# Doubled tails for the on-chip transposes, moved b2 sums and a held-back QK product in a fused attention and MLP kernel

## The chip, the cores and the metric

The kernel runs on one NeuronCore of a Trainium2 chip. The metric is the device time of one launch in microseconds (us). Work is spread over TensorE (PE: matmuls, with its weight loads shown as PEld), VectorE (DVE), ScalarE (ACT), GpSimd (POOL) and SyncE (SP), which here only issues DMAs. Every engine runs its own instructions strictly in the order in which they stand, and waits for other engines through semaphores: an instruction that waits holds up everything behind it on its engine.

## The reference

One transformer block over 2048 rows of 576 columns. Attention has 32 heads of 18 columns; each row looks at eight rows, itself and those 2, 4, ... 14 rows back.

```python
qkv = layernorm(x) @ wqkv                               # 576 -> 3 x 576
logits = einsum("bhsd,bhswd->bhsw", q, kg) * scale       # kg: k at s, s-2, ..., s-14
o = einsum("bhsw,bhswd->bhsd", softmax(logits), vg) @ wo
h = x + o
h2 = h + gelu(layernorm(h) @ w1 + b1) @ w2 + b2          # 576 -> 4608 -> 576
```

## The kernel before

The rows are split into 16 tiles of 128, tile j holding rows j, j + 16, j + 32 and so on, so that the eight rows of a window lie in tiles of the same parity at the same partition (or one partition up, which is what the "halo" copies supply). Even tiles are projected first, then odd ones. Attention takes the tiles in the order 14, 12, 10, ... 0, 15, ... 1, two at a time; these pairs are the groups: group 0 is tiles 14 and 12, group 1 is 10 and 8, group 2 is 6 and 4, group 3 is 2 and 0. All engines but the DMA rings follow an order that is written out by hand; pools only add the waits.

*Projection* (`qkv_duo`, line 297; matmuls at L216). 24 visits of two products each. A product has a first phase and a second; the second waits for a marker, a GpSimd no-op that itself waits for the first phase (L226), so **markers stand in GpSimd's queue** with everything else there. PSUM pairs A, B and C go round; a product can begin when ScalarE has emptied the pair used three products earlier (L311). Pair D takes transposes and the output product `wo_duo`. The tables `after`, `between` and `hooks` say what each engine gets behind, inside and within a visit.

*Transposes on TensorE* (`transpose_in`, L181). For groups 0's two tiles, the attention output o (`tr_o`) and the normalized h (`tr_h`) are turned in 64-row halves: five 128-column blocks, two matmuls each. The fifth block starts at column 448, and as its lower 64 rows of output must hold columns 512 to 575 once more, two more matmuls of 64 x 64 follow. `tr_x` leaves these two out. From group 1 on, the same turning is done by DMA: a store to the DRAM tile `td` (L198, L199), then a transposing read (L204 and L434 for o into `oT`, L498 for normalized h into `hnT`).

*Attention on VectorE.* For a tile: QK product (L343, `att_qk_a`), four halving additions (L352, `att_qk_add`) and one more into `logits` (L359), maximum and subtraction (L365, L366), on ScalarE the exponential (L384), denominators (L392 to L394), PV product (L398), additions (L404), last one into `q_all` (L405), which then holds o. `halo(j, 1)` and `halo(j, 2)` (L338, issued by SyncE) bring rows of k and v into the ring slot of tile j. They overwrite what the QK or PV product of that tile has read, so they wait for it; they also wait for the store of tile j to DRAM (`store_halo`, L295).

*LN2 of group 0* (`ln2`, L147 to L170): statistics on VectorE, the power -0.5 on GpSimd (L161), `ln_nmr` on VectorE (L170), normalization on ScalarE (L174). `add_b2` (L504) writes h + b2 on VectorE to `x_all`, where the output is summed. *LN2 from group 1 on* (`ln2_act`, L479 to L483, and `ln2_send`): statistics on ScalarE, the power on GpSimd (L482). `root` can make the next QK product wait for that power (lines 345 to 347); it is set for every tile but those of group 1.

*MLP.* `mlp1` multiplies a group's `hnT` by w1 in four visits (L216, `pm`), ScalarE applies gelu (L562), `mlp2` multiplies by w2 (L581 for groups 0 and 1; from group 2 on `mlp2_fast`, L669, with a scheme of seven products for eight, whose sums VectorE makes at L639 and L649). While group k runs here, attention of group k + 2 and LN2 of group k + 1 run beside it. For k = 0 the tables call tiles c = 10, d = 8, e = 6, f = 4; for k = 1 c = 6, d = 4, e = 2, f = 0. `ia` and `ib` are lists of calls put ahead of a row of `mlp2` of the group's first and second tile, `m1[v]` of a visit of `mlp1`.

SyncE's queue for k = 0, `ia[19]`, is in this order: `put_b2` of tile 8, stores of tiles 4 and 2 to DRAM, `halo(4, 1)`, then the store of tile 8's normalized h to `td`, then the two transposing reads into `hnT`:

```python
ia[19] = [lambda d=d: wo_visit((d, "A"), fill=True), c_(ln2_h, d), c_(ln2_act, d), c_(put_b2, d), c_(att_qk_a, f),
          c_(halos, 2), c_(halo, f, 1), c_(ln2_send, d), c_(ln2_ins, c, d), c_(att_qk_rest, f, 1), c_(exps, e, f)]
```

Of the kernel before, what the change touches and what calls it, by code (L numbers as in the profile page):

```python
# [17 lines left out]
def kernel(  # L18
# [157 lines left out]

    def transpose_in(pair, src, twice=True):
        def turn(rows, kt, c):
            for r in range(2):
                block = src[half_rows(r), c:c + P if rows.start is None else D]  # L180
                nc.tensor.matmul(pair[rows, r, kt * HP:(kt + 1) * HP], lhsT=block, rhs=ident[half_rows(r), half_rows(r)],  # L181
                                 start=True, stop=True, skip_group_check=True)

        for kt in range(KT):
            turn(slice(None), kt, min(kt * P, D - P))
        if twice:
            turn(half_rows(0), KF, KF * P)

# [76 lines left out]
    def tr_x(j, tag):  # L265
        pair = psum_pair(tag or "CAB"[(ring_pos[0] + 1) % 3], "xt_pt")
        transpose_in(pair, q_all[:, j, :], False)
# [26 lines left out]
    def store_halo(j, ts=slice(0, 2)):  # L294
        nc.sync.dma_start(out=kv_dram[j, 1:P + 1, ts, :], in_=kv_ring[j % 2][:, j // 2, ts, :])  # L295

# [42 lines left out]

    root = [None]  # L340

    def att_qk_a(j):
# [12 lines left out]
    def att_qk_b(j, i, skip=0):  # L355
        side[j] = i
        out = logit_of([j])[:, 0]
        att_qk_add(j, ((0, 0, 9), (0, 0, 4), (0, 0, 2), (0, 0, 1))[skip:])
# [63 lines left out]
    def tr_o(j, tag):  # L422
        pair = psum_pair(tag, "o_pt")
        transpose_in(pair, q_all[:, j, :])
        nc.scalar.copy(**turned(new_oT(j), pair))
# [4 lines left out]
    def send_o(j):  # L430
        o_sent[j] = dma_out(q_all[:, j, :])

    def read_o(j):
        nc.sync.dma_start_transpose(out=new_oT(j)[:], in_=o_sent.pop(j)[:])  # L434

# [39 lines left out]
    def ln2_act(j):  # L475
        h = h_of[j]
        y = sb.tile([P, D], BF16, tag="hn", name="hn", bufs=2)
        nmean, var, rstd = (sb.tile([P, 1], F32, tag=f"ln2_{t}", name=f"ln2_{t}", bufs=2) for t in ("nmean", "var", "rstd"))
        nc.scalar.activation(out=y[:], in_=h[:], func=ACT.Identity, scale=-1.0 / D, accum_out=nmean[:])  # L479
        nc.scalar.activation(out=y[:], in_=h[:], func=ACT.Square, bias=nmean[:], accum_out=var[:])  # L480
        nc.scalar.activation(out=var[:], in_=var[:], func=ACT.Identity, scale=(1.0 + EPS) / D, bias=eps2[:])  # L481
        ins = nc.gpsimd.tensor_tensor(out=rstd[:], in0=var[:], in1=mhalf[:], op=ALU.pow).ins  # L482
        root[0] = ins if j not in GROUPS[1] else None  # L483
        hn[j] = (h, rstd, nmean, y)
# [35 lines left out]

    def ln2_hn(j):
        h, rstd, nmr = hn[j]
        hn[j] = sb.tile([P, D], BF16, tag="hn", name="hn", bufs=2)
        ln_apply_act(hn[j][:], h[:], rstd[:, 0:1], nmr[:, 0:1])

    def hnT_slot(j):
# [5 lines left out]
    def tr_h(j, tag):  # L532
        pair = psum_pair(tag, "h_pt")
        transpose_in(pair, hn.pop(j)[:])
        nc.scalar.copy(**turned(hnT_slot(j), pair))
# [145 lines left out]
    def c_(fn, *a):  # L681
        return lambda: fn(*a)
# [100 lines left out]
    with tc.manual_schedule(engines={ENG.PE, ENG.Activation, ENG.DVE, ENG.SP, ENG.Pool}):  # L783
# [132 lines left out]
        for n, v in enumerate((19, 19, 20, 20, 21, 22)):  # L916
# [5 lines left out]
            3: [c_(ln1_even_rstd, 6, 7), c_(ln1_stats, 8)],  # L922
            4: [c_(ln1_rstd, 8), c_(ln1_stats, 9), c_(ln1_stats, 10, c_(ln1_bias, 8))],
            5: [c_(ln1_act, 8, 0), c_(ln1_rstd, 9), c_(ln1_bias, 9), c_(att_qk_a, A[0])],
# [7 lines left out]
            13: [c_(ln1_act, 10, 1), c_(in_x, 2), c_(out_x, 3)],  # L932
            14: [c_(att_pv, A[1]), c_(in_x, 3), c_(load, b2_bc, B_b2.partition_broadcast(P))],
            15: [c_(halo, A[1], 2)],
            17: [c_(ln2, A[0]), c_(att_qk_a, A[2])],
            18: [c_(ln2_rstd, A[0]), c_(add_b2, A[0]), c_(ln2_bias, A[0]), c_(halo, A[2], 1), c_(att_qk_add, A[2], ((0, 0, 9),))],
            19: [c_(ln2, A[1])],
            20: [c_(ln2_rstd, A[1]), c_(add_b2, A[1]), c_(ln2_bias, A[1]), c_(att_qk_rest, A[2], 0, 1)],
        }
# [3 lines left out]
            18: {1: [c_(tr_o, A[1], "D")]},  # L943
            19: [c_(ln2_hn, A[0])],
            21: [c_(ln2_hn, A[1])],
            22: [c_(att_exp, A[2])],
# [43 lines left out]
        def halos(n):  # L990
            for _ in range(min(n, len(pending_halo))):
                store_halo(pending_halo.pop(0))

# [11 lines left out]
        for k, g in enumerate(GROUPS):  # L1005
# [11 lines left out]
            if k == 0:  # L1017
                m1[0] += [c_(halos, 1), c_(load_w2, 6), c_(att_qk_a, d), c_(att_qk_rest, d, 1), c_(halo, d, 1)]
                mid[0] = {1: [c_(exps, d)]}
                m1[1] = [c_(pv_t, c), c_(pv_t, d), c_(att_qk_a, e), c_(halo, e, 1)]  # L1020
                late_wo = wo_duo(c, "B")
                ia[0] = [c_(ln2_h, c), c_(ln2_act, c), c_(put_b2, c), c_(ln2_send, c), c_(att_qk_rest, e, 0)]
                ia[19] = [lambda d=d: wo_visit((d, "A"), fill=True), c_(ln2_h, d), c_(ln2_act, d), c_(put_b2, d), c_(att_qk_a, f),
                          c_(halos, 2), c_(halo, f, 1), c_(ln2_send, d), c_(ln2_ins, c, d), c_(att_qk_rest, f, 1), c_(exps, e, f)]
                ib[0] = [c_(finish_out, g[0]), c_(out_sum, g[0]), c_(att_den, e, f), c_(pv_sum, e), c_(send_o, e)]
                ib[8] = [c_(read_o, e), c_(out_store, g[0])]
            elif k == 1:
                m1[0] += [c_(pv_sum, d), c_(send_o, d)]
# [100 lines left out]
```

## Time and profile before

| what | value |
|---|---|
| median of 3 runs | 361.9 us (361.39 to 362.56) |
| the profiled execution | 361.35 us, of which its span is 359.6 us |
| granted TensorE clock | 1.000 |
| busy: PE, PEld, DVE, ACT, POOL | 353.4, 292.4, 296.3, 234.8, 46.5 us |
| matmuls L216 pq (projection) | 864, 283 ns each, overlapping |
| transposes L181 of o and of h | 24 and 24, 190 ns each in 64 x 128 form, 213 ns in 64 x 64 form |
| b2 sums L504 | 2, 0.75 us each |
| power of LN2 (L161, L482) | 27 instructions, 22.6 us |

The span is the time from the first to the last instruction; 1.75 us of the profiled execution lie outside it. Matmuls are pipelined, so their durations overlap: the pace of TensorE is read from the distance between starts, not from the busy time. In the lines that follow the first number is the start in us from the start of the span and the second the length; a bracket gives the idle time of that engine just before, and what ended it.

### The profile page before, as it was taken

What the parts mean: (1) busy time and instruction counts of PE and PEld (TensorE: products, weight loads), DVE (VectorE), ACT (ScalarE), POOL (GpSimd) and SP (SyncE); (2) the same over time, 40 slices, a digit from 0 to 9 for tenths busy, and PEclk for the clock granted to TensorE, in tenths of its full rate; (3) what the DMA queues carried; (4) which work ended last, traced back from release to release, by engine and by line L of the source; (5) the groups of instructions that cost most, each with busy time, mean ns of one, the idle gap of its engine ahead of it and who ended that gap; (6) DMA issues with size and microseconds to landing.
All of it is one profiled execution on the core that took longest, in us unless ns stands there. A gap on an engine that the chain in (4) does not pass through costs nothing.

```text
span 359.6 us, 11560 instructions
## 1 busy us (share of the span) xinstructions
PE 353.4 (98%) x4942; PEld 292.4 (81%) x4942; DVE 296.3 (82%) x417; ACT 234.8 (65%) x519; POOL 46.5 (13%) x61
## 2 busy tenths in 40 slices
PE   7999999999999999999999999999999999999996
PEld 3778977887789877887788778877887788778874
DVE  5999999999989999997799899989998998520431
ACT  4879756897647783668566956695669566706620
POOL 2241004000112020201110202021102110210000
PEclk9999999999999999999999999999999999999999
DMA  7996789973447494731563655344636254273001
GB/s 241 339 285 192 202 223 300 369 246 73 136 88 119 142 239 81 137 71 51 94 101 76 98 124 85 90 96 110 88 90 100 57 86 58 54 122 50 4 1 33
DMA packets 62980, 46.29 MB, mean 129 GB/s; under 512 B 32192, under 2 KB 60736, under 8 KB 62928
## 3 DMA queue, kind: packets, MB, share of 16 engines
q1 hardware_dynamic: 58960, 41.50, 44.0%
q0 software_dynamic: 3744, 3.84, 9.8%
q8 instruction: 38, 0.62, 0.8%
q10 hardware_dynamic: 224, 0.22, 0.2%
q14 instruction: 14, 0.11, 0.1%
HBM read 23.38 MB, written 12.42 MB: 100 GB/s over the span
## 4 chain that ended last, share of the span: by engine, by line
PE 76%; DVE 14%; DMA 3%; SPq 2%; ACT 2%; issue 1%; POOL 0%; POOLq 0%; ACTq 0%
PE pm L216 34%; PE po L669 25%; PE pq L216 8%; PE po L581 5%; PE pw L216 4%; DVE prod L352 2%; DVE ln_stats L148 2%; DVE prod L343 2%; DVE prod L398 1%; DMA x_all<-in_A_x_dram 1%; DVE prod L404 1%; ACT h_all L562 1%; SPq L104 1%; DMA hnT<-td 1%; DMA oT<-td 1%
## 5 line engine op out<-in xcount | busy, mean ns | idle before, releaser
L216 PE MATMUL pm<-hnT,w_sb 64*128 64x256 bf16 x2304 | 143.0, 269 | 0.2 <-DMA hnT<-td 0.2
L562 ACT ACTIVATE h_all<-pm,b_sb 128x256 f16<-128x256 f32 (+1 forms) x288 | 108.6, 496 | 51.2 <-PE pm L216 50.6
L216 PEld LDWEIGHTS <-w_sb 64*128 64x128 bf16 x2304 | 113.6, 94 | 13.5 <-issue 1.9
L669 PEld LDWEIGHTS <-h_all 128*128 128x128 f16 x480 | 46.2, 98 | 13.7 <-issue 1.6
L216 PE MATMUL pq<-wq_sb,xnT 64*128 64x288 bf16 x720 | 54.9, 283 | 1.3 <-ACT xnT L272 0.5
L216 PEld LDWEIGHTS <-xnT 64*128 64x128 bf16 x864 | 44.0, 94 | 10.6 <-ACT xnT L272 1.2
L352 DVE TENSOR_TENSOR prod<-prod 128x2304 bf16<-128x2304 bf16 (+1 forms) x64 | 44.2, 691 | 2.0
L343 DVE TENSOR_TENSOR prod<-kv_ring,q_all 128x4608 bf16<-128x4608 bf16 x16 | 40.9, 2555 | 3.1 <-POOL ln_rstd L482 2.5
L398 DVE TENSOR_TENSOR prod<-kv_ring,probs 128x4608 bf16<-128x4608 bf16 x16 | 40.9, 2558 | 1.1 <-DMA kv_ring<-kv_dram 0.6
L216 PE MATMUL pm<-hnT,w1h_sb 64*128 64x256 bf16 x288 | 39.5, 269 | 0.0
L669 PE MATMUL po<-w2a_sb,h_all 128*128 128x288 bf16 (+1 forms) x262 | 35.8, 286 | 0.0
L404 DVE TENSOR_TENSOR prod<-prod 128x2304 bf16<-128x2304 bf16 (+1 forms) x32 | 33.9, 1058 | 1.1
L581 PEld LDWEIGHTS <-h_all 128*128 128x128 bf16 x288 | 27.9, 98 | 7.9 <-issue 1.0
L669 PEld LDWEIGHTS <-kv_ring 128*128 128x128 f16 x252 | 24.6, 98 | 6.3
L581 PE MATMUL po<-w2a_sb,h_all 128*128 128x288 bf16 x224 | 28.5, 286 | 0.0
L216 PE MATMUL pq<-wqh_sb,xnT 64*128 64x288 bf16 x144 | 27.6, 283 | 0.0
L771 POOL DMA_DIRECT2D x_all<-o_sb x12 | 10.7, 890 | 124.6 <-PE pw L216 71.8
L482 POOL TENSOR_TENSOR ln_rstd<-ln_var,mhalf 128x1 f32<-128x1 f32 x13 | 9.3, 718 | 81.9 <-ACT ln_var L481 81.9
L669 PE MATMUL po<-w2b_sb,h_all 128*128 128x288 bf16 (+1 forms) x122 | 19.7, 286 | 0.2 <-DVE h_all L649 0.2
L649 DVE TENSOR_TENSOR kv_ring<-h_all 128x1536 f16<-128x1536 f16 (+3 forms) x9 | 6.8, 761 | 15.6 <-ACT h_all L562 15.6
L216 PE MATMUL pw<-wo_sb,oT 64*128 64x288 bf16 x256 | 19.5, 283 | 0.1
L161 POOL TENSOR_TENSOR ln_rstd<-ln_veps,mhalf 128x1 f32<-128x1 f32 (+2 forms) x14 | 13.3, 965 | 47.6 <-DVE ln_veps L155 31.1
(107 smaller groups left out, 399.3 us busy)
## 6 DMA issues: line engine op xcount, KB each, us to landing
w_sb<-in_B_w_dram SPq DMA_DIRECT2D x6, 768.0 KB, 6.3
kv_ring<-kv_dram SPq DMA_DIRECT2D x28, 144.0 KB, 2.4
kv_dram<-kv_ring SPq DMA_DIRECT2D x13, 288.0 KB, 4.1
x_all<-in_B_b_dram SPq DMA_DIRECT2D x15, 144.0 KB, 3.7
w2a_sb<-in_B_w_dram SPq DMA_DIRECT2D x2, 1008.0 KB, 8.0
td<-q_all SPq DMA_DIRECT2D x14, 144.0 KB, 1.8
td<-hn SPq DMA_DIRECT2D x14, 144.0 KB, 1.8
x_all<-h POOLq DMA_DIRECT2D x14, 144.0 KB, 4.8
```

Of the source, the lines that this page charges most:

```text
L148: nc.vector.bn_stats(out=stats[:, i, c, :], in_=src[:, c * HALF:(c + 1) * HALF])
L161: nc.gpsimd.tensor_tensor(out=rstd[:], in0=veps[:], in1=mhalf[:].to_broadcast([P, n]), op=ALU.pow)
L216: last = nc.tensor.matmul(duo["g"][r ^ swap][i], lhsT=lhsT, rhs=rhs, start=(swap == 0 and i == 0 and kt == 0), stop=(swap == 1 and kt == K ...
L343: ins = nc.vector.tensor_tensor(out=prod[:], in0=k_ring[j % 2], in1=q_all[:, j, :].unsqueeze(1) .to_broadcast([P, W, D]), op=ALU.mult).ins
L352: nc.vector.tensor_tensor(out=prod[:, :, o * H:o * H + n], in0=prod[:, :, a * H:a * H + n], in1=prod[:, :, c * H:c * H + n], op=ALU.add)
L398: nc.vector.tensor_tensor(out=prod[:].rearrange("p w (d h) -> p w d h", h=H), in0=v_ring[j % 2].rearrange("p w (d h) -> p w d h", h=H), in ...
L404: nc.vector.tensor_tensor(out=prod[:, 0:n, :], in0=prod[:, 0:n, :], in1=prod[:, n:2 * n, :], op=ALU.add)
L482: ins = nc.gpsimd.tensor_tensor(out=rstd[:], in0=var[:], in1=mhalf[:], op=ALU.pow).ins
L562: pace[0] = nc.scalar.activation(out=hT(grp)[:, f, 0:N], in_=ps[:, r, i * N:(i + 1) * N], func=ACT.Gelu_apprx_tanh, bias=b1_sb[:, f:f + 1] ...
L581: nc.tensor.matmul(banks[half], lhsT=hT(grp)[:, f, i * P:(i + 1) * P], rhs=w2_rows(f)[:, half * HALF:(half + 1) * HALF], start=(f == 0), s ...
L669: nc.tensor.matmul(bank, lhsT=l, rhs=r, start=start, stop=stop, skip_group_check=True)
L771: nc.gpsimd.dma_start(out=x_of(j), in_=o_of.pop(j), accum_op=ALU.add)
```

## The change

The two extra matmuls of each of the four transposes of group 0 go. In their place somebody writes columns 512 to 575 twice into a new tile `tail`, from which the fifth block is turned: ScalarE for o of tile 14 (behind visit 14), VectorE for o of tile 12 (behind its PV sums), ScalarE for the two normalized h (a second normalization of 128 columns right behind the first). The two b2 sums move from group 0's LN2 to the place behind the PV sums of tile 8. In the second half of group 0's `mlp2` the sum h of tile 8 comes ahead of the last logits, maximum and subtraction of tile 6, and the QK product of tile 4 waits for the power of tile 8's LN2. In group 1, o of tile 4 is sent ahead of `halo(4, 2)`, the store of output tile 14 goes two visits later, and the seven stores of odd tiles wait for the transposing read of o. In the projection `ln_bias` of the first four odd tiles moves ahead of the last statistics. Numbers in `after` are visits.

```diff
-    def transpose_in(pair, src, twice=True):
-        def turn(rows, kt, c):
-            for r in range(2):
-                block = src[half_rows(r), c:c + P if rows.start is None else D]
-                nc.tensor.matmul(pair[rows, r, kt * HP:(kt + 1) * HP], lhsT=block, rhs=ident[half_rows(r), half_rows(r)],
-                                 start=True, stop=True, skip_group_check=True)
-        for kt in range(KT):
-            turn(slice(None), kt, min(kt * P, D - P))
-        if twice:
-            turn(half_rows(0), KF, KF * P)
+    def transpose_in(pair, src, tail=None):
+        for kt in range(KT):
+            c = min(kt * P, D - P)
+            block = tail[:].rearrange("p r c -> p (r c)") if kt == KF and tail is not None else src[:, c:c + P]
+            for r in range(2):
+                nc.tensor.matmul(pair[:, r, kt * HP:(kt + 1) * HP], lhsT=block[half_rows(r)],
+                                 rhs=ident[half_rows(r), half_rows(r)], start=True, stop=True, skip_group_check=True)
+    def twice(src):
+        return src[:, KF * P:D].unsqueeze(1).to_broadcast([P, 2, HP])
+    def new_tail(key):
+        tails[key] = qp.tile([P, 2, HP], BF16, tag="tail", name="tail", bufs=2)
+        return tails[key][:]
+    def o_tail(j, copy):
+        copy(out=new_tail(("o", j)), in_=twice(q_all[:, j, :]))
...
-        root[0] = ins if j not in GROUPS[1] else None
+        root[0] = ins if j != GROUPS[1][0] else None
...
-    def ln2_hn(j):
+    def ln2_hn(j, tail=False):
...
+        if tail:
+            ln_apply_act(new_tail(("h", j)), twice(h), rstd[:, 0:1], nmr[:, 0:1])
...
-            4: [c_(ln1_rstd, 8), c_(ln1_stats, 9), c_(ln1_stats, 10, c_(ln1_bias, 8))],
+            4: [c_(ln1_rstd, 8), c_(ln1_stats, 9), c_(ln1_bias, 8), c_(ln1_stats, 10)],
...
-            14: [c_(att_pv, A[1]), c_(in_x, 3), c_(load, b2_bc, B_b2.partition_broadcast(P))],
+            14: [c_(o_tail, A[0], nc.scalar.copy), c_(att_pv, A[1]), c_(o_tail, A[1], nc.vector.tensor_copy), c_(in_x, 3), c_(load, b2_bc, B_b2.partition_broadcast(P))],
...
-            18: [c_(ln2_rstd, A[0]), c_(add_b2, A[0]), c_(ln2_bias, A[0]), c_(halo, A[2], 1), c_(att_qk_add, A[2], ((0, 0, 9),))],
+            18: [c_(ln2_rstd, A[0]), c_(ln2_bias, A[0]), c_(halo, A[2], 1), c_(att_qk_add, A[2], ((0, 0, 9),))],
...
-            20: [c_(ln2_rstd, A[1]), c_(add_b2, A[1]), c_(ln2_bias, A[1]), c_(att_qk_rest, A[2], 0, 1)],
+            20: [c_(ln2_rstd, A[1]), c_(ln2_bias, A[1]), c_(att_qk_rest, A[2], 0, 1)],
...
         def halos(n):
             for _ in range(min(n, len(pending_halo))):
-                store_halo(pending_halo.pop(0))
+                ins = store_halo(pending_halo.pop(0))
+                if o_read[0] is not None:
+                    tc.add_manual_dep(ins, o_read[0].name, sync_dep, reason="stores behind the read of o")
...
-                m1[1] = [c_(pv_t, c), c_(pv_t, d), c_(att_qk_a, e), c_(halo, e, 1)]
+                m1[1] = [c_(pv_t, c), c_(pv_t, d), c_(add_b2, g[0]), c_(add_b2, g[1]), c_(att_qk_a, e), c_(halo, e, 1)]
-                ia[0] = [c_(ln2_h, c), c_(ln2_act, c), c_(put_b2, c), c_(ln2_send, c), c_(att_qk_rest, e, 0)]
-                ia[19] = [lambda d=d: wo_visit((d, "A"), fill=True), c_(ln2_h, d), c_(ln2_act, d), c_(put_b2, d), c_(att_qk_a, f),
+                ia[0] = [c_(ln2_h, c), c_(ln2_act, c), c_(put_b2, c), c_(ln2_send, c), c_(att_qk_add, e, ADDS)]
+                ia[19] = [lambda d=d: wo_visit((d, "A"), fill=True), c_(ln2_h, d), c_(ln2_act, d), c_(put_b2, d), c_(att_qk_rest, e, 0, 4), c_(att_qk_a, f),
...
-                ib[8] = [c_(read_o, e), c_(out_store, g[0])]
+                ib[8] = [c_(read_o, e)]
             elif k == 1:
-                m1[0] += [c_(pv_sum, d), c_(send_o, d)]
+                m1[0] += [c_(att_pv_sum, d), c_(send_o, d), c_(halo, d, 2)]
-                m1[3] += [c_(att_qk_a, f), c_(halo, f, 1), c_(att_qk_add, f, ((0, 0, 9), (0, 0, 4)))]
+                m1[3] += [c_(out_store, GROUPS[0][0]), c_(att_qk_a, f), c_(halo, f, 1), c_(att_qk_add, f, ADDS[:2])]
```

More of the change, by code (lines that the diff above doesn't have):

```diff
@@ L174, in ln_apply_act @@
         nc.scalar.activation(out=dst, in_=src, func=ACT.Identity, scale=rstd, bias=nmr)
-    def transpose_in(pair, src, twice=True):
-        def turn(rows, kt, c):
+    def transpose_in(pair, src, tail=None):
+        for kt in range(KT):
+            c = min(kt * P, D - P)
+            block = tail[:].rearrange("p r c -> p (r c)") if kt == KF and tail is not None else src[:, c:c + P]
             for r in range(2):
-                block = src[half_rows(r), c:c + P if rows.start is None else D]
-                nc.tensor.matmul(pair[rows, r, kt * HP:(kt + 1) * HP], lhsT=block, rhs=ident[half_rows(r), half_rows(r)],
-                                 start=True, stop=True, skip_group_check=True)
-        for kt in range(KT):
-            turn(slice(None), kt, min(kt * P, D - P))
-        if twice:
-            turn(half_rows(0), KF, KF * P)
+                nc.tensor.matmul(pair[:, r, kt * HP:(kt + 1) * HP], lhsT=block[half_rows(r)],
+                                 rhs=ident[half_rows(r), half_rows(r)], start=True, stop=True, skip_group_check=True)
+    tails = {}
+    def twice(src):
[5 more added lines that the diff above has]
+        copy(out=new_tail(("o", j)), in_=twice(q_all[:, j, :]))
     def turned(dst, pair, k0=0, k1=KT):
@@ L266, in tr_x @@
         pair = psum_pair(tag or "CAB"[(ring_pos[0] + 1) % 3], "xt_pt")
-        transpose_in(pair, q_all[:, j, :], False)
+        transpose_in(pair, q_all[:, j, :])
         if EVEN.index(j) % 2 == 0:
@@ L294, in store_halo @@
     def store_halo(j, ts=slice(0, 2)):
-        nc.sync.dma_start(out=kv_dram[j, 1:P + 1, ts, :], in_=kv_ring[j % 2][:, j // 2, ts, :])
+        return nc.sync.dma_start(out=kv_dram[j, 1:P + 1, ts, :], in_=kv_ring[j % 2][:, j // 2, ts, :]).ins
     def qkv_duo(j, t):
@@ L340 @@
     root = [None]
+    ADDS = ((0, 0, 9), (0, 0, 4), (0, 0, 2), (0, 0, 1))
     def att_qk_a(j):
@@ L357, in att_qk_b @@
         out = logit_of([j])[:, 0]
-        att_qk_add(j, ((0, 0, 9), (0, 0, 4), (0, 0, 2), (0, 0, 1))[skip:])
+        att_qk_add(j, ADDS[skip:])
         nc.vector.tensor_tensor(out=out, in0=prod[:, :, 0:H], in1=prod[:, :, 8 * H:9 * H], op=ALU.add)
@@ L423, in tr_o @@
         pair = psum_pair(tag, "o_pt")
-        transpose_in(pair, q_all[:, j, :])
+        transpose_in(pair, q_all[:, j, :], tails.pop(("o", j)))
         nc.scalar.copy(**turned(new_oT(j), pair))
@@ L431, in send_o @@
         o_sent[j] = dma_out(q_all[:, j, :])
+    o_read = [None]
     def read_o(j):
-        nc.sync.dma_start_transpose(out=new_oT(j)[:], in_=o_sent.pop(j)[:])
+        o_read[0] = nc.sync.dma_start_transpose(out=new_oT(j)[:], in_=o_sent.pop(j)[:]).ins
     pw_of, o_sent = {}, {}
@@ L533, in tr_h @@
         pair = psum_pair(tag, "h_pt")
-        transpose_in(pair, hn.pop(j)[:])
+        transpose_in(pair, hn.pop(j)[:], tails.pop(("h", j)))
         nc.scalar.copy(**turned(hnT_slot(j), pair))
@@ L943 @@
             18: {1: [c_(tr_o, A[1], "D")]},
-            19: [c_(ln2_hn, A[0])],
-            21: [c_(ln2_hn, A[1])],
+            19: [c_(ln2_hn, A[0], True)],
+            21: [c_(ln2_hn, A[1], True)],
             22: [c_(att_exp, A[2])],
```

## The prediction

> **What bounds the kernel now.** I read the chain of work that ended last first, then the engines' timelines around its joints. TensorE takes 76% of the chain and from 125.5 to 338 us it never pauses: a delay that reaches it there is added to the end, and a gain must come before 125 us.
>
> ```profile
> PE 76%; DVE 14%; DMA 3%; SPq 2%; ACT 2%; issue 1%; POOL 0%; POOLq 0%; ACTq 0%
> ...
> 93.92 2.48 DVE prod L343
> 96.42 1.37 DVE prod L352
> 97.79 0.32 SPq L338
> ...
> 98.21 0.98 SPq L198
> ...
> 102.15 2.92 DMA hnT<-td
> ...
> 105.21 15.66 PE pm L216 x284
> 120.87 2.85 DMA oT<-td
> ```
>
> The reader sees that group 1's MLP (105.21) waits for VectorE, then for SyncE's halo copy of tile 4 (97.79), then for tile 8's normalized h (98.21) and its transposing read.
>
> ```profile
> 12.53 0.31 PE L181 MATMUL xt_pt<-ident,q_all 64*128 64x64 bf16 x10
> 12.68 0.65 PE L216 MATMUL pq<-wq_sb,xnT 64*128 64x288 bf16 x8
> ...
> 45.26 0.67 PE L216 MATMUL pq<-wq_sb,xnT 64*128 64x288 bf16 x8
> 45.75 0.31 PE L216 MATMUL pq<-wqh_sb,xnT 64*128 64x288 bf16 x2
> 45.87 0.48 PE L181 MATMUL o_pt<-ident,q_all 64*128 64x64 bf16 x12
> 46.28 0.66 PE L216 MATMUL pq<-wq_sb,xnT 64*128 64x288 bf16 x7
> ```
>
> Ten transposes hold TensorE from 12.53 to 12.68 (0.15 us), twelve, two of them 64 x 64, from 45.87 to 46.28 (0.41 us).
>
> ```profile
> 45.16 0.46 DVE L405 TENSOR_TENSOR q_all<-prod 128x576 bf16<-128x576 bf16 x1
> ...
> 60.55 0.75 DVE L504 TENSOR_TENSOR x_all<-h,x_all 128x576 bf16<-128x576 f32 x1
> 61.75 0.16 DVE L170 SCALAR_TENSOR_TENSOR ln_nmr<-ln_mv,ln_rstd 128x1 f32<-128x1 f32 x1 [0.45 <-POOL ln_rstd L161]
> ```
> ```profile
> 44.38 1.19 ACT L311 ACTIVATE kv_ring<-pq 128x576 bf16<-128x576 f32 x2 [1.00 <-PE pq L216]
> ```
> ```profile
> 60.71 1.00 POOL L161 TENSOR_TENSOR ln_rstd<-ln_veps,mhalf 128x1 f32<-128x1 f32 x1 [3.62 <-DVE ln_veps L155]
> ...
> 96.03 0.76 POOL L482 TENSOR_TENSOR ln_rstd<-ln_var,mhalf 128x1 f32<-128x1 f32 x1 [4.50 <-ACT ln_var L481]
> ```
>
> o of tile 14 is there at 45.16 + 0.46 = 45.62, while ScalarE empties projection pairs from 44.38. The second b2 sum lies inside the wait for the power; VectorE has no other idle time from 19 to 101 us. Last, TensorE's own small waits:
>
> ```profile
> 83.59 0.48 PEld L216 LDWEIGHTS <-oT 64*128 64x128 bf16 x10 [0.35 <-DMA oT<-td]
> ...
> 123.76 1.46 PEld L216 LDWEIGHTS <-oT 64*128 64x128 bf16 x26 [0.39 <-DMA oT<-td]
> ```
>
> By starts TensorE loses 0.25 us at 83.6, 0.35 at 105.2 (rows end at 104.86) and 0.26 at 123.8 (at 123.50 it could go on).
>
> **Part 1, to 66.55 us.** Four turns lose 0.26 us each: 1.0 us. ln_bias ahead of statistics frees ScalarE 0.6 us earlier and ends a TensorE gap of 0.40 us at 25.20. Little of this stays. ScalarE's tail copy of tile 14 stands ahead of the two evacuations that begin at 44.38, and waits for 45.62. It costs 0.29 us by a line through ScalarE's rows of 36 and 256 columns (0.19 and 0.42 us, the bounds). The first evacuation (0.65 us) then begins near 45.87 and ends at 46.52; the product that starts at 45.26 needs that pair, so it starts near 46.55, 1.29 us late, whatever was won earlier. The shorter turn leaves +1.03 at 46.28. Now waits shrink. The second turn needed pair D from tile 14's sum h (VectorE, 52.92). VectorE's tail copy of tile 12 costs 0.2 (0.15 for its 1-column rows, 0.42 for 256 columns from PSUM): h ends at about 53.2, TensorE comes at 53.9, so no wait, and +0.68 after the shorter turn. The third turn was followed by 0.15 us behind a marker queued after the power; that goes, as does 0.26: +0.3. The fourth must wait for ScalarE's tail (0.29 behind hn), which also delays an evacuation that had 0.2 us to spare: +0.3 at 66.55 (0 to 0.6). The wait at 83.6 takes 0.25 of it: nothing lasting.
>
> VectorE's own chain matters more. The power of tile 12 took 1.00 us with a b2 sum beside it; four powers with no two-operand VectorE work beside them took 2.10 us, 0.53 each. I take 0.53, that being the state after the change: VectorE reaches this power 0.13 late: the tail copy waits for the end of o (52.25 instead of the overlapped 52.17) and takes its 0.2, and about 0.1 comes back because ln_nmr of tile 14 no longer stands behind a b2 sum. So the power runs from 60.84 to 61.37 and ln_nmr comes at 61.42 instead of 61.75: -0.33 (+0.13 if 1.00 stays). The Trainium skill, "SBUF — State Buffer", section "SBUF: two separate sides", says that a GpSimd operation reading SBUF and a VectorE one with two SBUF inputs exclude each other for their whole length; the 1.00 us row, ending 0.4 after the sum, fits. Without that rule, the shift would be the +0.13, and the total 0.46 higher, 363.1.
>
> **Part 2, 85 to 105 us.** Both b2 sums now stand in VectorE's busy stretch: 2 x 0.67 (starts one after the other) = 1.34. QK of tile 6: 85.45 - 0.33 + 1.34 = 86.46, +1.0. Sum h of tile 10: 88.93, ScalarE's LN2 of tile 10 (88.71 to 92.67 before, 3.96 us) ends at 93.67. Ahead of logits, sum h of tile 8 comes at about 92.5 (before 93.17), but ScalarE takes it up only at 93.67 (before 93.95): of the 0.67 us won by the swap 0.28 is left. The marker of tile 8's output product, queued behind tile 10's power (90.86 + 1.0), holds TensorE 0.2 us; the next wait hides it. Power of tile 8: 96.03 - 0.28 = 95.75, ready at 96.28. **Now QK of tile 4 waits for it**: 96.32 instead of 93.83. Behind it VectorE is late by 2.5 us, and SyncE's halo copy of tile 4, which overwrites what this product reads, can't be issued before its end: 96.32 + 2.55 + 0.03 = 98.90, where the store's landing set 97.79. Tile 8's h, ready at 97.7, is queued behind that copy: 99.32 instead of 98.21, +1.1. Its issue took 0.98 us where others of this form take 0.34; if the longer time came from the stores then landing, 0.64 is won back. So the read into hnT lands +0.47 to +1.1 later; between ends so far apart I take 0.8: TensorE starts at 106.0.
>
> What the hold-back buys is small: the power of tile 8 took 0.76, of which 0.23 above 0.53.
>
> **Part 3, from 105 us.** SyncE no longer has an output store and a halo copy ahead of the sending of tile 4's o. VectorE finishes this o at 114.70 + 2.5 = 117.2; the next halo copy waits for a QK product to 119.7, so the read can be issued at 120.1 and land at 122.95 (before 123.72). TensorE comes at 123.50 + 0.8: the wait of 0.26 goes, +0.54 is left. The seven stores, held to that landing, issue from 123 to 128.4 (before 122.13 to 127.5), the two output stores to 129.8, then come two loads; tile 6's h wants the queue at 131.64 + 2.2, so they cost nothing. VectorE, less its 0.29 us of waiting at 121.25, makes sums h of group 2 2.2 us late; the second read into hnT, issued at 137.4, is issued at 139.6 and lands 2.9 to 4.6 us later (both measured), 142.5 to 144.2; TensorE wants it at 143.21 + 0.54 = 143.75. Between 0 and 0.45, I take 0.15. After 162.4 VectorE had waited 2.12 us for TensorE, which takes up the 2.2. Sum: 0.8 - 0.26 + 0.15 = **+0.7**. On the profiled execution: 361.35 + 0.7 = 362.05; this execution lies 0.55 below the median, so by the median **362.6 us**.
>
> **Rivals.** *A, the VectorE delay reaches TensorE again.* The 2.5 us also move the exponential of tiles 6 and 4 (to 103.7), the copy of group 0's first output (to 106.4) and the GpSimd DMA behind it (1.05 us, to 107.8), and the marker that TensorE needs at 107.39 + 0.8 = 108.2 is queued behind that DMA: 0.4 us of cover where there were 2.2. If it starts 0.6 us after its release, as others do, 0.2 is lost; with the 1.1 end in part 2 and hnT at 144.2 or a little later, +1.5 to +2.2: about 363.8. For it: three small covers at once; against: each holds by itself at my mid values. *B, not slower:* the b2 sums and the hold-back end before SyncE needs tile 4's halo. Place: the copy at 97.79. It decides if QK of tile 4 ends by then, so starts by 95.2, 1.1 us earlier than I have. Then the store of tile 8's h goes at 98.2 or 97.9, the 0.35 at 105.2 shrinks, the 0.26 at 123.8 goes: 361.9 - 0.3 to 0.6, 361.4. Against: VectorE has no idle time in which 1.34 us of sums could hide. *C, the tail copy on ScalarE isn't absorbed:* if the power of tile 12 and the DMA of tile 10's o do not come earlier and ScalarE's evacuations stay crowded, 0.5 more reaches 83.6 us; but the wait at 105.2 hides what is below 0.8, so 362.9.
>
> **How the numbers follow.** Forecast 0.55 (own range 362.1 to 363.3), A 0.25, B 0.12, C 0.08. The median of three runs before spans 1.2 us, so within 0.3% (1.09 us: 360.8 to 363.0) is what can't be told from no change. The forecast lies three quarters within and one quarter above, A is above, B half below (runs differ) and half within, C half and half. Slower: 0.14 + 0.25 + 0.04 = 0.43; faster 0.06; same 0.51. Range 361.4 to 364.0: B's value below, A's end above.
>
> **What would show it.** Right: 10 transposes in 0.15 us; ScalarE idle up to a tail copy at 45.65 and TensorE idle over 0.8 us near 45; QK of tile 4 at about 96.3, released by GpSimd; halo copy of tile 4 near 98.9; first pm of group 1 near 106.0 on hnT; no wait for oT of tile 4. Wrong: QK of tile 4 before 95.2, or the store of tile 8's h ahead of 98.2; an hnT wait at group 2 over 0.5 us; TensorE gaps after 162 us.

## The result, and the profile after

The changed kernel takes 363.38 us (median of 7 runs, 362.37 to 363.5), the kernel before beside it on the same chip 361.57 us (361.25 to 362.56). The ratio is 1.0039, with a 95% interval of 1.0025 to 1.0053: 0.9 to 1.9 us slower. The middle lies above the 0.3% that I set as the limit of no change, the lower end just below it. I had forecast 362.6 us, +0.7; the time is inside the range, and by the ratio (+1.4) about twice as far from the old one as forecast. The profiled execution took 363.14 us with a span of 361.3 (before: 361.35 and 359.6), so its difference, 1.79, has to be found in the trace.

The chain of work that ended last, its shares and its joints around group 1's MLP (start, length, what):

```profile
PE 69%; DVE 15%; DMA 6%; issue 3%; SPq 2%; ACT 2%; POOL 1%; POOLq 0%; DVEq 0%; ACTq 0%
```
```profile
79.39 2.13 DMA td<-q_all
81.54 2.96 DMA oT<-td
84.55 0.79 PE pw L224 x10
...
91.46 0.74 PE pw L224 x10
...
96.29 0.55 POOL ln_rstd L493
96.86 2.57 DVE prod L352
99.45 0.32 SPq L346
...
99.87 1.10 SPq L206
101.02 1.57 DMA td<-hn
...
103.94 3.08 DMA hnT<-td
...
107.16 17.86 PE pm L224 x324
125.02 2.20 PE pw L224 x36
127.22 17.75 PE po L594 x144
```

Group 1's MLP starts at 107.16 instead of 105.21, 1.95 later, through the same links as before: QK product, halo copy, sending of tile 8's h, read into `hnT`. TensorE's share of the chain falls from 76% to 69%, and GpSimd's power (96.29) stands in it. Behind 107.16 only 0.26 comes back: the output product at 125.02 follows the MLP without the old wait for `oT`. From there to the end everything is about 1.7 us later: 1.95 - 0.26 = 1.69 is the whole difference of the spans.

VectorE's timeline (start, length, line, operation; in brackets the idle time before and what ended it):

```profile
85.52 1.42 DVE L515 TENSOR_TENSOR x_all<-h,x_all 128x576 bf16<-128x576 f32 x2
86.86 2.55 DVE L352 TENSOR_TENSOR prod<-kv_ring,q_all 128x4608 bf16<-128x4608 bf16 x1
...
93.41 0.76 DVE L473 TENSOR_TENSOR h<-pw,x_all 128x576 f32<-128x576 f32 x1 [0.56 <-PE pw L224]
...
96.86 2.56 DVE L352 TENSOR_TENSOR prod<-kv_ring,q_all 128x4608 bf16<-128x4608 bf16 x1 [1.03 <-POOL ln_rstd L493]
```

Sum h of tile 8 (93.41) is taken ahead of the softmax maximum and yet comes later than before (93.17): it now waits 0.56 us for TensorE's output product. That product, in the kernel before and then in the changed one:

```profile
90.44 0.66 PE L216 MATMUL pw<-wo_sb,oT 64*128 64x288 bf16 x8
```
```profile
91.39 0.66 PE L224 MATMUL pw<-wo_sb,oT 64*128 64x288 bf16 x8
```

It starts 0.95 late, because TensorE took up the `oT` of tile 10 0.95 late (84.55 instead of 83.60). Two delays run side by side there. TensorE itself was 0.66 late since the projection (group 0's MLP starts at 67.21 instead of 66.55). And `oT` came 0.95 late: 0.18 from VectorE, as SyncE began to send that o at 79.00 instead of 78.82; 0.58 from the store, 2.54 us from its first issue to the issue of the read (81.54) instead of 1.96; and 0.19 from the read.

ScalarE's row shows a second chain that ends at the same moment:

```profile
93.30 0.87 ACT L174 ACTIVATE hn<-h,ln_nmean,ln_rstd 128x576 bf16<-128x576 f32 x1
```

ScalarE is through with tile 10 at 93.30 + 0.87 = 94.17, just when sum h of tile 8 ends (93.41 + 0.76), and goes on with tile 8 at 94.20. An earlier sum h alone would have won next to nothing. Behind this the QK product of tile 4 waits 1.03 us for the power.

The early part, TensorE, then ScalarE, then VectorE, then GpSimd:

```profile
46.40 0.67 PE L224 MATMUL pq<-wq_sb,xnT 64*128 64x288 bf16 x8 [0.57 <-ACT kv_ring L319]
46.89 0.30 PE L224 MATMUL pq<-wqh_sb,xnT 64*128 64x288 bf16 x2
47.01 0.30 PE L182 MATMUL o_pt<-ident,q_all 64*128 64x64 bf16 x8
47.12 0.21 PE L182 MATMUL o_pt<-ident,tail 64*128 64x64 bf16 x2
47.16 0.65 PE L224 MATMUL pq<-wq_sb,xnT 64*128 64x288 bf16 x7
```
```profile
45.50 0.30 ACT L195 COPY tail<-q_all 128x128 bf16<-128x128 bf16 x1 [1.73 <-DVE q_all L414]
45.71 1.18 ACT L319 ACTIVATE kv_ring<-pq 128x576 bf16<-128x576 f32 x2
```
```profile
47.57 2.56 DVE L407 TENSOR_TENSOR prod<-kv_ring,probs 128x4608 bf16<-128x4608 bf16 x1 [0.76 <-DMA kv_ring<-kv_dram]
...
61.95 0.16 DVE L170 SCALAR_TENSOR_TENSOR ln_nmr<-ln_mv,ln_rstd 128x1 f32<-128x1 f32 x1 [0.67 <-POOL ln_rstd L161]
```
```profile
61.35 0.56 POOL L161 TENSOR_TENSOR ln_rstd<-ln_veps,mhalf 128x1 f32<-128x1 f32 x1 [3.49 <-PE pq L224]
```

The turn takes 0.15 us (47.01 to 47.16) instead of 0.41. But ScalarE stands idle 1.73 us ahead of its tail copy, and the product that began at 45.26 begins at 46.40. VectorE waits 0.76 us at the PV product of tile 12, for a halo copy, where it had not waited before. So `ln_nmr` of tile 12 comes 0.20 late, although the power in front of it is down from 1.00 to 0.56 us.

That halo copy was not held up by a tail copy. SyncE issued it at 44.13 (before: 43.43), ahead of the first tail copy at 45.50, and was late already at its read into `xnT` (before, then after):

```profile
37.59 1.29 SPq L285 DMA_TRANSPOSE xnT<-xd  x1
```
```profile
38.32 1.29 SPq L293 DMA_TRANSPOSE xnT<-xd  x1
```

### The profile page after: what moved, and what is told of

Read it like the earlier page. It is cut to its first block, busy times and chain, and to the rows that moved or that the text cites. A ratio compares the mean times of both kernels' runs of the same rounds, so it can differ in the third digit from the quotient of the medians.

```text
span 361.3 us, 11548 instructions
## 1 busy us (share of the span) xinstructions
PE 352.5 (98%) x4934; PEld 295.8 (82%) x4934; DVE 296.3 (82%) x418; ACT 235.0 (65%) x522; POOL 45.8 (13%) x61
## 4 chain that ended last, share of the span: by engine, by line
PE 69%; DVE 15%; DMA 6%; issue 3%; SPq 2%; ACT 2%; POOL 1%; POOLq 0%; DVEq 0%; ACTq 0%
PE pm L224 34%; PE po L682 22%; PE po L594 6%; PE pw L224 5%; DVE prod L352 3%; DVE prod L361 3%; DVE ln_stats L148 2%; DMA hnT<-td 2%; PE pq L224 2%; DVE prod L407 1%; DMA x_all<-in_A_x_dram 1%; DVE prod L413 1%; ACT h_all L575 1%; SPq L104 1%; POOL ln_rstd L161 1%
## 5 line engine op out<-in xcount | busy, mean ns | idle before, releaser
L224 PEld LDWEIGHTS <-w_sb 64*128 64x128 bf16 x2304 | 116.9, 94 | 11.4 <-issue 2.7
```

The source lines that it names most:

```text
L224: last = nc.tensor.matmul(duo["g"][r ^ swap][i], lhsT=lhsT, rhs=rhs, start=(swap == 0 and i == 0 and kt == 0), stop=(swap == 1 and kt == K ...
```

## The experiments

All kernels ran in five rounds beside the kernel before. I give the ratio to it with its 95% interval, and microseconds from the ratio times 361.9. Single profiles differ by some tenths of a microsecond before 25 us already, so I compare places within a profile.

**The hold-back alone**, on the kernel before.

```diff
-        root[0] = ins if j not in GROUPS[1] else None
+        root[0] = ins if j != GROUPS[1][0] else None
```

> The kernel before, with the hold-back of tile 4's QK product alone. Theory (the hold-back costs, because SyncE's halo copy of tile 4 waits for that product and tile 8's h and tile 4's o stand behind it): QK of tile 4 starts near 96.6 instead of 93.83, halo copy near 99.2, tile 8's h sent near 99.6, first pm of group 1 near 106.5 instead of 105.21; VectorE is 2.8 us late from there, so the transposing read of tile 4's o, which in this order stands behind a halo copy and an output store, lands near 126 and TensorE waits more than 1 us there: total +1.3 to +2.9 us, about 363 to 364.4. Rival (the b2 sums and the tails are the cost, the hold-back is hidden): within 0.4 us of the kernel before.

1.0065 (1.0042 to 1.0089), +2.4 us. VectorE's timeline of this kernel:

```profile
94.79 0.75 DVE L462 TENSOR_TENSOR h<-pw,x_all 128x576 f32<-128x576 f32 x1
98.24 2.56 DVE L343 TENSOR_TENSOR prod<-kv_ring,q_all 128x4608 bf16<-128x4608 bf16 x1 [2.70 <-POOL ln_rstd L482]
```

VectorE idles 2.70 us. TensorE then waits three times: for `hnT` at 108.04, for `oT` (0.2 us at 126.5) and 1.31 us for group 2's `hnT`. The mechanism of my part 2 is there, and it can cost more than the whole change does. (The profiled execution had lost 1.6 us ahead of the edit: at 58.20 a b2 sum had waited 1.49 us for its load. Counted from the start of group 0's MLP, group 1's MLP is 1.2 us later than before, and the wait at group 2 adds 1.3.)

**The changed kernel without the hold-back** (the same line turned round).

> The changed kernel without the hold-back. Rival theory (only the queue of SyncE counts): QK of tile 4 starts near 95.8 instead of 96.86, halo copy 98.4, tile 8's h sent near 98.8, first pm of group 1 near 106.1 instead of 107.16: total -1.0 us, about 362.4. Theory (power and QK product exclude each other): the power of tile 8, wanted at 96.3, runs only when the QK product that began at 95.8 ends, so its row is 2 to 2.6 us long and ends near 98.9; tile 8's h is ready only near 100.2, the first pm of group 1 is at 107.2 to 107.5, and the total is that of the changed kernel within 0.4 us.

1.0021 (1.0005 to 1.0037), +0.8 us. The gain of about 0.65 lies between the two expectations, and the intervals overlap. The trace decides for the second one as to the cause; GpSimd, then TensorE at group 1:

```profile
96.79 2.43 POOL L493 TENSOR_TENSOR ln_rstd<-ln_var,mhalf 128x1 f32<-128x1 f32 x1 [3.28 <-ACT ln_var L492]
```
```profile
107.74 0.50 PE L224 MATMUL pm<-hnT,w_sb 64*128 64x256 bf16 x6 [1.26 <-DMA hnT<-td]
```

The QK product that began at 96.26 runs to 98.81, and the power, asked for at 96.79, ends at 99.22. Tile 8's h isn't sent earlier (100.48, in a profile that runs 0.5 to 0.6 behind at this place), and TensorE still waits 1.26 us.

**The changed kernel with tile 4's halo copy behind tile 8's h** in SyncE's queue.

```diff
-c_(halos, 2), c_(halo, f, 1), c_(ln2_send, d), c_(ln2_ins, c, d), c_(att_qk_rest, f, 1)
+c_(halos, 2), c_(ln2_send, d), c_(ln2_ins, c, d), c_(halo, f, 1), c_(att_qk_rest, f, 1)
```

> The changed kernel with SyncE's halo copy of tile 4 behind the sending of tile 8's h and the two reads into hnT. Both theories: tile 8's h goes at 98.1 instead of 99.87, the hnT read lands before or near 105.8, where TensorE's rows end, and first pm of group 1 starts near 105.8 to 106.1 instead of 107.16. Theory 1 (SyncE's queue at 99 is the only cost): total -1.1 to -1.3, about 362.2. Theory 2 (VectorE's lateness of 2.6 us is a second limit just behind it): the read of tile 4's o is still issued near 122.1 and lands near 124.9, so TensorE, coming at 123.5 to 123.8, waits there 1 us or more, and the total is within 0.4 us of the changed kernel.

1.0020 (1.0001 to 1.0038), +0.7 us. TensorE's timeline:

```profile
105.37 0.61 PE L224 MATMUL pm<-hnT,w_sb 64*128 64x256 bf16 x8
...
125.33 0.67 PE L224 MATMUL pw<-wo_sb,oT 64*128 64x288 bf16 x8 [1.48 <-ACT h_all L575]
...
145.35 0.61 PE L224 MATMUL pm<-hnT,w_sb 64*128 64x256 bf16 x8 [0.51 <-DMA hnT<-td]
```

The queue did cost the 1.2 us: at 105.37 there is no wait any more. But 1.48 us are waited at 125.33 and 0.51 at 145.35. The bracket names a gelu that stood in the same place relative to TensorE in the changed kernel, without a wait; what is late is the read of tile 4's o, issued at 122.17 and 2.8 to 3.1 us from landing. Most of the gain is taken by the next link, as the second theory said, though not all of it by the medians. VectorE even waited 1.92 us more at the PV product of tile 4, for a halo copy issued at 109.2, beside two GpSimd DMAs issued from 108.49 on; that these slowed it wasn't tried.

**The changed kernel with the b2 sums back** beside group 0's LN2 (the two `add_b2` moved to where they were).

> The changed kernel with both b2 sums back beside group 0's LN2. Theory (the sums cost 1.4 us of VectorE where it has no idle time, and everything to the sending of tile 8's h follows): QK of tile 6 near 85.5 instead of 86.86, power of tile 8 near 95, QK of tile 4 near 95.5 instead of 96.86, halo copy 98.1, tile 8's h sent at 98.5, first pm of group 1 near 105.8 to 106 instead of 107.16, no wait for tile 4's o: total -1.2 to -1.4 against the changed kernel, about 362.0. Rival (the hold-back alone makes the loss, the sums are hidden by waits of VectorE): first pm of group 1 within 0.3 of 107.16 and the total within 0.3 us of the changed kernel. The power of tile 12 should be near 1.0 us again by the exclusion, 0.56 without it.

1.0034 (1.0018 to 1.0050), +1.2 us: no gain that can be told. VectorE:

```profile
86.25 2.56 DVE L352 TENSOR_TENSOR prod<-kv_ring,q_all 128x4608 bf16<-128x4608 bf16 x1
...
93.38 0.76 DVE L473 TENSOR_TENSOR h<-pw,x_all 128x576 f32<-128x576 f32 x1 [1.13 <-PE pw L224]
...
96.84 2.56 DVE L352 TENSOR_TENSOR prod<-kv_ring,q_all 128x4608 bf16<-128x4608 bf16 x1 [1.03 <-POOL ln_rstd L493]
```

VectorE comes 0.6 earlier and gives it back as a longer wait for tile 8's output product. This product, not the sums, sets tile 8's h here: TensorE starts it at 91.36 (91.39 in the changed kernel, 90.44 before), because it came late out of the projection and out of the wait for `oT` of tile 10. ScalarE is done with tile 10 0.6 us earlier here, at 93.56; in the changed kernel the two end together. My theory fell.

**The b2 sums alone**, on the kernel before.

```diff
-c_(add_b2, A[0]), 
-c_(add_b2, A[1]), 
-c_(pv_t, c), c_(pv_t, d), c_(att_qk_a, e)
+c_(pv_t, c), c_(pv_t, d), c_(add_b2, g[0]), c_(add_b2, g[1]), c_(att_qk_a, e)
```

> The kernel before with only the two b2 sums moved behind tile 8's PV sums. Theory (they cost VectorE 1.34 us where it has no idle time, less the 0.7 that their old place cost the one behind tile 14 and 0.45 of a shorter power): the power of tile 12 takes 0.55 us, QK of tile 6 starts 0.1 to 0.4 us later than before, QK of tile 4 the same, and the total is 0 to +0.5 us. Rival (as I predicted, 1.0 us later at QK of tile 6): +0.8 to +1.2 us there, first pm of group 1 up to 0.3 later, the read of tile 4's o 1 us later and a total of +0.8 to +1.2 us.

1.0004 (0.9984 to 1.0024): -0.6 to +0.9 us. Its profile lies 0.8 us above its median, with a wait of 1.08 us at the QK product of tile 8 that the others lack. Less that wait and 0.15 of a later start, QK of tile 6 is 0.75 later than before, which speaks for my forecast of that place rather than for the smaller figure expected here. The time can't be told from no change.

**Group 1's edits alone**, on the kernel before.

```diff
-                store_halo(pending_halo.pop(0))
+                ins = store_halo(pending_halo.pop(0))
+                if o_read[0] is not None:
+                    tc.add_manual_dep(ins, o_read[0].name, sync_dep, reason="stores behind the read of o")
...
-                ib[8] = [c_(read_o, e), c_(out_store, g[0])]
+                ib[8] = [c_(read_o, e)]
-                m1[0] += [c_(pv_sum, d), c_(send_o, d)]
+                m1[0] += [c_(att_pv_sum, d), c_(send_o, d), c_(halo, d, 2)]
-                m1[3] += [c_(att_qk_a, f)
+                m1[3] += [c_(out_store, GROUPS[0][0]), c_(att_qk_a, f)
```

> The kernel before with the edits of group 1 alone (o of tile 4 sent ahead of the halo copy, output store of tile 14 two visits later, seven stores behind the read of o). Theory: the read of tile 4's o goes about 1 us earlier, TensorE's wait of 0.26 us for it goes, nothing else changes before 105: total -0.1 to -0.4 us. Rival (the stores, issued later, hold up the sending of group 2's h): a wait of TensorE for hnT at group 2 and a total of 0 or more.

0.9982 (0.9970 to 0.9995): -0.65 us, 361.20 against 361.95. The output products follow without a break:

```profile
123.07 0.67 PE L216 MATMUL pw<-wo_sb,oT 64*128 64x288 bf16 x8
123.56 0.30 PE L216 MATMUL pw<-woh_sb,oT 64*128 64x288 bf16 x2
123.69 0.67 PE L216 MATMUL pw<-wo_sb,oT 64*128 64x288 bf16 x8
```

The wait for `oT` is gone and group 2 starts without one.

**Group 1's edits and the later halo copy**, on the kernel before.

> The kernel before with the edits of group 1 and with SyncE's halo copy of tile 4 behind the sending of tile 8's h and the reads into hnT. VectorE is on time here, unlike in the changed kernel. Theory: tile 8's h goes at 98.0 to 98.1 and its issue takes 0.34 instead of 0.98 us, the hnT wait of 0.35 us goes, and the wait for tile 4's o too: total -0.4 to -0.7 us. Rival (the later halo copy, or a later copy for tile 6's v colliding with GpSimd's DMAs, delays the PV product of tile 4, as when VectorE was late): a VectorE wait of 1 us or more near 110 and a total of -0.2 or more.

0.9979 (0.9966 to 0.9993), -0.75 us: no more than without the later copy. Tile 8's h went at 98.72 with 0.34 us, as expected, but then the second store took 0.95, and from the first issue to the read it was 2.56 us, as in the kernel without this step (2.55). Set against the sum h of tile 8 (93.85 here, 93.45 there) it went 0.3 us earlier, so the copy ahead of it had held it up by little. The total lies at the edge of the theory's -0.4 to -0.7, but that any of it comes from the later copy isn't shown.

**b2 put in by DMAs**, on that kernel: no sums on VectorE, two GpSimd DMAs instead.

```diff
-c_(add_b2, A[0]), 
-c_(add_b2, A[1]), 
+                m1[0] += [c_(put_b2, c0) for c0 in g] + [c_(halos, 1), ...
+                m1[1] = [c_(accumulate_hs, *g), c_(pv_t, c), c_(pv_t, d), ...
```

> As the one before it, and the two b2 sums of group 0 not on VectorE at all: b2 is put into the output by a DMA and h is added by a GpSimd DMA, as in the groups behind. Theory (VectorE's chain to tile 8's h is what counts): the power of tile 12 takes 0.55 us, QK of tile 6 starts 1.0 to 1.2 us earlier than before (near 84.4), tile 8's h is sent 0.5 to 1 us earlier, and the total is 0.3 to 0.7 us below the kernel without this step, about -0.8 to -1.3 us against the kernel before. Rival (TensorE's own work sets the time there): total within 0.2 us of the kernel without this step.

1.0117 (1.0090 to 1.0144), +4.2 us, a miss of both theories by my placing of the DMA:

```profile
75.54 1.97 POOL L512 DMA_DIRECT2D x_all<-h  x2 [14.79 <-DMA x_all<-in_B_b_dram]
```
```profile
76.11 2.36 PE L216 MATMUL pm<-hnT,w_sb 64*128 64x256 bf16 x40 [3.80 <-POOLq L226]
```

GpSimd waited for b2 to land until 75.5, the markers stood behind it, and TensorE waited 3.80 us for one.

**The tails and equal turns alone**, without `ln_bias`, on the kernel before.

```diff
+            14: [c_(o_tail, A[0], nc.scalar.copy), c_(att_pv, A[1]), c_(o_tail, A[1], nc.vector.tensor_copy), ...
+            19: [c_(ln2_hn, A[0], True)],
+            21: [c_(ln2_hn, A[1], True)],
```

> The kernel before with the five equal transposes and the four tail copies alone. Theory (the end hangs on VectorE's chain from 60 us, which the tail copy of tile 12 and a power of 1.0 us beside the b2 sum leave 0.1 to 0.3 us later, and what TensorE wins is waited away at 83.6 and 105.2): total 0 to +0.5 us against the kernel before. Rival (the 1.0 us of shorter turns lasts): -0.4 to -1.0 us. In the trace: turns of 0.15 us, TensorE idle 0.3 to 1.0 us near 46 behind ScalarE's tail copy, ln_nmr of tile 12 about 0.1 to 0.3 later, first pm of group 1 at the same time as before or up to 0.4 later.

1.0013 (0.9996 to 1.0030), +0.5 us (-0.1 to 1.1). TensorE waits 0.87 us at 46.81; the four shorter turns bring nothing to the end.

**The changed kernel without part 2**: tails, turns, `ln_bias` and group 1's edits; b2 sums, order of tile 8's h and hold-back as before.

> The changed kernel with b2 sums, order of tile 8's h and hold-back as before: so tails, ln_bias and group 1's edits are left. Theory (parts add): tails alone +0.5, group 1 alone -0.65, so -0.4 to +0.1 us against the kernel before; the loss of the whole change then lies in the part from 85 to 105 us. Rival (tails and ln_bias in the projection are the loss): +0.8 us or more.

1.0022 (0.9997 to 1.0046), +0.8 us, against group 1's edits alone at 0.9982: +1.45 us from tails, turns and `ln_bias`, and the rival is nearer. The profile of this kernel lies 1.5 us above its median and shows where such an execution loses it (DMA view from 94 to 104 us: issue, KB each, us to landing; then SyncE):

```profile
td<-hn SPq DMA_DIRECT2D x1, 144.0 KB, 4.3
```
```profile
98.61 0.38 SPq L206 DMA_DIRECT2D td<-hn  x1
99.04 0.42 SPq L207 DMA_DIRECT2D td<-hn  x1
103.16 2.53 SPq L509 DMA_TRANSPOSE hnT<-td  x2
```

Tile 8's h is sent early, and lands late.

**No b2 sums at all**, with old turns and with new ones. Both have group 1's edits and the later halo copy; the second adds tails, new turns and `ln_bias`. The outputs of tiles 14 and 12 lack h + b2, so these two kernels only serve to measure.

```diff
-c_(ln2_rstd, A[0]), c_(add_b2, A[0]), 
-c_(ln2_rstd, A[1]), c_(add_b2, A[1]), 
+c_(ln2_rstd, A[0]), 
+c_(ln2_rstd, A[1]), 
```

> The kernel before with the edits of group 1 and the later halo copy of tile 4, and both b2 sums of group 0 left out, so that the outputs of tiles 14 and 12 lack their h. Theory (VectorE's chain sets the time up to 105): power of tile 12 takes 0.55 us, QK of tile 6 starts 1.0 to 1.2 us earlier relative to the projection, tile 8's h is sent 0.5 to 0.8 earlier, first pm of group 1 about 0.3 to 0.6 earlier, as TensorE's own rows end 0.35 before the old start: total -0.3 to -0.6 us against the kernel with the sums, about -1.0 to -1.4 against the kernel before. Rival (TensorE's own work sets it already): within 0.2 us of the kernel with the sums.

> As the one before it (both b2 sums left out), with the five equal transposes, their tails and the ln_bias move. Theory (with VectorE off the chain TensorE's work counts, and the shorter turns are worth 0.3 to 0.7 us after the wait behind ScalarE's tail copy): -0.3 to -0.7 us against the kernel without sums and with the old turns. Rival (the tail copies cost ScalarE and VectorE as much as TensorE wins): within 0.2 us of it or above it.

Old turns: 0.9961 (0.9949 to 0.9973), -1.4 us. New turns: 1.0008 (0.9991 to 1.0024), +0.3 us. The intervals lie apart: tails, turns and `ln_bias` cost 1.7 us here, where I expected them to win 0.3 to 0.7, and the rival's "above it" holds. SyncE of the two, old turns first, and VectorE with the new ones:

```profile
97.39 0.34 SPq L198 DMA_DIRECT2D td<-hn  x1
97.77 1.09 SPq L199 DMA_DIRECT2D td<-hn  x1
100.08 2.54 SPq L500 DMA_TRANSPOSE hnT<-td  x2
```
```profile
98.28 0.34 SPq L206 DMA_DIRECT2D td<-hn  x1
98.67 0.43 SPq L207 DMA_DIRECT2D td<-hn  x1
102.25 2.54 SPq L509 DMA_TRANSPOSE hnT<-td  x2
```
```profile
47.58 2.56 DVE L407 TENSOR_TENSOR prod<-kv_ring,probs 128x4608 bf16<-128x4608 bf16 x1 [0.43 <-DMA kv_ring<-kv_dram]
```

With the new turns the sending comes 0.89 later; 0.24 of this lies in an execution that was behind at 25 us already, 0.43 is the wait shown for a halo copy, and the remaining 0.2 is VectorE's tail copy. The other 1.28 of the 2.17 us at the read is the store itself: 3.97 us from issue to read instead of 2.69. TensorE's 1.0 us of shorter turns doesn't show up anywhere behind 66 us.

## Why the prediction was partly right

*What bounds the kernel.* Right for the changed kernel: every gain or loss that reached the end came before 125 us, and 107.16 to 125.02 to 127.22 are the joints where it was decided. In two experiments TensorE waited behind 125 us too, for group 2's `hnT` (1.31 and 0.51 us).

*Part 1, its early steps.* Right in nearly all: turns of 0.15 and 0.14 us for o (those of h took 0.24 and 0.39, the last one behind ScalarE's tail, as I had said); ScalarE idle up to its tail copy at 45.50 (said: 45.62); the stalled product at 46.40 (46.55); VectorE's tail copy 0.19 (0.2); a power of 0.56 (0.53) once no sum ran beside it. TensorE came to the MLP 0.66 late (67.21) where I had +0.3, just over my 0 to 0.6. Two sizes behind it: the tail of a normalized h takes ScalarE 0.48 us, not 0.29, as it normalizes 128 columns anew.

*Part 1, its end: wrong.* "The wait at 83.6 takes 0.25 of it: nothing lasting", together with "-0.33" for `ln_nmr` of tile 12, is the step that failed. I put part 1 at nothing. Taken over kernels that are otherwise the same, tails, turns and `ln_bias` cost 1.45 us (0.5 to 2.4) and 1.7 us (0.9 to 2.5); without `ln_bias` 0.5 (-0.1 to 1.1).

The trace shows two places. First, in place of -0.33 it has +0.20: the PV product of tile 12 started 0.56 late, behind the halo copy that it needs, while my sum followed only VectorE's own instructions. Without these 0.56 the shift would by my estimate have been -0.36, next to my figure. Second, TensorE took up `oT` of tile 10 0.95 late and so brought tile 8's output product late. I had TensorE 0.3 late and a wait of 0.25 to hide it; it was 0.66 late, and `oT` was late as well, by 0.77 more than VectorE's 0.18. With `oT` on time about 0.4 (0.66 - 0.25) would by my estimate have been left.

Why the halo copy and the sending of o are late stays open. SyncE issued the halo copy 0.08 to 0.94 us behind the end of the PV product of tile 14 in the seven kernels without tails, and 0.51 to 1.54 in the seven with them; the PV product of tile 12 waited in five of these seven, 0.28 to 0.82 us, and in none of the others. But the copy stands ahead of the first tail copy, so no wait behind a tail explains it, and the kernel without `ln_bias` has it late too (1.15 us behind the PV product; read into `xnT` at 38.08). The new tile `tail` also takes room in SBUF, so that other tiles may lie elsewhere; neither that nor `ln_bias` alone was tried. My rival C had one part of this, a tail copy that isn't absorbed, but only 0.3 above the forecast, because I let the wait at 105.2 cover it.

*Part 2.* The mechanism is there as forecast: QK of tile 4 released by GpSimd (96.86, said 96.32), the halo copy behind it (99.45, said 98.90), tile 8's h behind that (99.87, said 99.32). The price is real: the hold-back alone cost 2.4 us on the old kernel. Two terms were mis-sized. Of the 0.47 to 1.1 at `hnT` I took 0.8, hoping that the long issue would shorten; it took 1.10, the read came 1.79 later, and TensorE started 1.95 later. In the profile my sum reads 1.95 - 0.26 + 0 = 1.69: the term of 0.8 is the one that was off. Of the missing part 0.5 was there before the queue: tile 8 went on at 94.20, where I had 93.67, as sum h of tile 8 came at 93.41 and not at 92.5, behind TensorE's late product, and ScalarE was done with tile 10 no earlier. With the sums put back nothing was won. "What the hold-back buys is small", 0.23 us, fell too: with tile 8's h ahead of the maximum the power would fall inside the QK product and take 2.43 us. The profile before held the warning: its power of tile 14, at 54.28 beside the QK product of 54.12, took 2.80 us. The Trainium skill, "SBUF — State Buffer", section "SBUF: two separate sides", has the two engines exclude each other for the length of the operation. The row of 2.43 us agrees with it more plainly than the 1.00 that I had. The marker, for which I had 0.2 us, cost nothing: from first to second phase of tile 8's product it was 1.31 us, before 1.32.

*Part 3.* Right in sign, and small as a gain: the wait for `oT` went. Measured alone the edits gave 0.65 us (0.2 to 1.1), where I had 0.26. Group 2 started without a wait in the changed kernel (I had 0.15). My 0.26 can't be told from the measured value.

*The sum.* I had 0.8 - 0.26 + 0.15 = +0.7. The runs have about +1.45 for part 1 with `ln_bias`, -0.65 for part 3, and what is left of +1.4 for part 2: 0.6 us, with an uncertainty of about 1. So my 0.8 for part 2 by itself can't be told wrong by these runs, and that the time fell into my range is in part luck: a cost that I had at nothing was partly offset by a gain larger than mine. Rival A was as near in size (363.8), but not in place: no marker behind the GpSimd DMA held TensorE. Rival B is out: QK of tile 4 started at 96.86, not by 95.2.

The parts don't add up, as they work on limits that lie side by side. Without the hold-back the power is late; without the queue's copy `oT` is late; without the sums TensorE's product is late. Each of these three removals from the changed kernel left 0.7 to 1.2 us of its 1.4.

The best of these kernels with the whole computation are group 1's edits alone, or with the later halo copy, at 0.9982 and 0.9979, faster than both the old and the changed kernel.

## What to carry to other kernels

Before you book a gain on the busiest engine, follow every copy that refills what the next engine reads, and ask how much room it has: here a halo copy issued some tenths later than before took away all that a shorter power had won. And see where the replacement of an instruction stands: here 1.0 us of TensorE was bought with copies on ScalarE and VectorE that stood ahead of work that TensorE and VectorE's own chain were waiting for. An instruction moved ahead in a queue wins only if its input is there; the sum taken ahead of a maximum then waited for the product that it adds. Where several links end within a microsecond of each other, measure each edit alone and in company before keeping it.

## What the hardware showed that I had not expected

The same GpSimd power took 0.55 us with VectorE idle, 0.76 when a QK product ended 0.35 us behind its start, 1.00 beside a b2 sum, and 2.43 inside a QK product: in the last three it ended 0.41 us behind VectorE's operation. So did a power of 2.80 us in the profile before (54.28, beside the QK product of 54.12 with 2.55 us), which I had passed over.

The store of tile 8's normalized h (144 KB and 16 KB) took 2.4 to 2.9 us from its first issue to the issue of the read in ten profiles, and 3.2 to 4.6 in four. It doesn't help if SyncE gets rid of both issues quickly: with 0.38 and 0.42 us the landing took 4.3, with 1.09 for one of them the whole took 2.69. All four slow ones were kernels with tails, but three others with tails were not slow. What makes the difference stays open.
